# Packed attention and gated MLP on one core: batch 2's attention held behind batch 0's last gate, batch 1's parts laid out again, weights narrowed later

## The chip, the cores and the metric

The kernel runs on one NeuronCore of a Trainium2 chip. Its engines are TensorE (PE, matmuls; "PEld" is its weight load), VectorE (DVE), ScalarE (ACT), GpSimd (POOL) and SyncE (SP, whose queue "SPq" issues all DMAs here). Each engine works through its own queue in order; a waiting instruction holds up all behind it. Time is device microseconds (us) of the whole kernel; the figure compared is the median over runs.

## The reference

Eight batches, eight heads, 576 tokens, head size 64. For each batch and head, 32 packed queries `p` attend to `k` and `v`; then every token's `q` attends to the 32 packed results, which serve as keys and values. The result, turned to tokens x 512, goes through a gated MLP with 2048 inner features.

```python
def sm_attn(qq, kk, vv):
    s = scale * np.matmul(qq, kk.transpose(0, 1, 3, 2))
    s = s - np.max(s, axis=-1, keepdims=True)
    a = np.exp(s)
    a = a / (np.sum(a, axis=-1, keepdims=True) + 1e-09)
    return np.matmul(a, vv)
p_packed = sm_attn(p, k, v)
out = sm_attn(q, p_packed, p_packed)
# x = out as (4608, 512)
h = x @ w_in
g = h * np.clip(h + 3.0, 0.0, 6.0) / 6.0
return g @ w_out
```

The two weight matrices arrive as 64-bit floats, so their words are loaded as pairs of 32-bit integers and turned into 32-bit floats on the chip ("narrowed").

## The kernel before

**Folding.** The second attention's product with the packed values is folded into the MLP: `m = p_packed x w_in` is made per batch (for batch 0 in `u_m0`, 128 inner features at a time; for the others in `u_m`, 512 at a time), and the first product is `m` times the attention weights `a`. Both are split into a high and a low part (`m_hi`, `m_lo`, `a_hi`, `a_lo`), so a first product is three matmuls for each of two head groups. The gate follows: a Relu on ACT (L994 for batch 0), min and multiply on DVE (L995). The second product multiplies the gated tile with w_out.

**Three stages.** `first_attention` (from L499) does batch 0's attention, with an order written out by hand. `first_moe` (from L934) does batch 0's MLP in 16 steps, one for each 128 inner features, and carries three other things between its matmuls: loading the weights, narrowing them, and batch 1's attention. Then a loop over batches 1 to 7 does each batch's MLP with the next batch's attention in between (`moe`, `fill`, `attention`); it uses w_out split into a high and a low part (`split_w_out`, L173 on ACT and L175 on DVE).

**A step f of `first_moe`**, on PE: 12 matmuls of the first product (`gemm1`, L491), 8 of `u_m0(f+1)` (L207), then 8 of the second product of step f-1 (L947). The first product's PSUM tile has one buffer, so step f+1's first product waits for step f's gate on DVE; it also waits for `m_lo(f+1)` (L220, DVE, after `m_hi`, L218, ACT). `u_m0` and all parts of batch 1's attention share two PSUM banks (`att_ps`), and a half of `s1` or `s2` takes both.

**Narrowing** (`narrowed`, L131) of one 128x512 tile is two operations on ACT (L143, L145), two on DVE (L151, L153) and an add on POOL (L157). w_in(f) must be narrowed before `u_m0(f)`, w_out(f) before the second product of f. Raw tiles of w_in have three buffers, those of w_out two; tiles 2 and 3 have places of their own. `w_in_step` and `w_out_step` are generators: `step(x, n)` takes n operations of one, `rest(x)` all that are left.

**Batch 1's attention** is the table that `first_parts` (L452) returns: a row for each step, with three places: before the first product, after the gate, and after the second product. `ld` issues four DMAs (L227) for one pair of heads into one of two `nat` buffers, `tn` turns such a tile on DVE (L406) and so frees the buffer; `load_p` issues four (L247), `load_v` five (L263). `s1` (scores of the packed queries, softmax), `et` (transposes of the weights), `pv` (their product with v), `ppt` (transpose of the result) and `s2` (scores of all queries, softmax, turn, split) are generators of which each `go` takes the next piece.

**What sets the order.** Inside `first_attention` and `first_moe` the order on PE, DVE, ACT and POOL is the program's; in `first_moe` on SP too. What is traced outside (batch 2's attention, the splits of w_out, most of batch 1's MLP) is placed by a planner, which works with estimated times and puts such instructions between the hand-ordered ones where it thinks an engine is free. `tc.issue_after(ins)` keeps every instruction of its block that runs on the engine of `ins` behind `ins` in that engine's queue. `first_moe` returns `gate`, the last step's two gate instructions, and the splits are held behind them.

The three spots around which the prediction turns:

```python
rest(in_(f + 2))                       # L990, ahead of the gate
gate = [nc.scalar.activation(...)]     # L994
gate.append(nc.vector.scalar_tensor_tensor(...))   # L995
if f:
    rest(m_(f + 1))
attend(f, 1)
rest(out_(f + 1), out_(f + 2))
```

## Time and profile before

| what | value |
|---|---|
| time, median of 3 runs (lowest to highest) | 778.28 us (777.43 to 779.56) |
| profiled execution, time of its own | 780.75 us |
| its span, first to last instruction | 778.9 us |
| mean granted clock of PE | 0.987 |
| busy: PE, weight loads, DVE, ACT, POOL | 751.4, 575.6, 359.7, 378.0, 252.9 us |
| DMA: packets, bytes | 191203, 55.95 MB |
| first instruction of batch 1's first product (L864) on PE | 162.79 us |

A timeline row reads: start, length, engine, line, operation, output<-inputs, shapes, count, and in brackets how long the engine had stood idle before it and what released it. A row of groups gives the count, then busy us and mean ns, then the idle time before them. Times inside the span are from its start.

### The profile page before, as it was taken

The page shows a single profiled execution, that of the slowest core. Times are in us where ns is not written, and L with a number is a line of the kernel's source. Part 1 is how long each engine was busy: PE and PEld are TensorE (multiplying, and loading weights), DVE is VectorE, ACT ScalarE, POOL GpSimd, SP SyncE. Part 2 cuts the span into 40 slices and gives each one's busy share as a digit, 9 for nine tenths or more (in the row PEclk, how much of TensorE's full clock was granted, in tenths as well). Part 3 has the DMA queues.
Part 4 walks back from the last instruction along what each step waited for, and adds up shares of the span by engine and source line. Part 5 has one row for each costly group of instructions (what it writes and reads, how often), then busy time and mean ns, then how long its engine had stood idle before and what let it go on. Part 6 is the DMA issues. An engine that isn't in the chain of part 4 may idle for free.

```text
span 778.9 us, 13851 instructions
## 1 busy us (share of the span) xinstructions
PE 751.4 (96%) x5133; PEld 575.6 (74%) x5133; DVE 359.7 (46%) x746; ACT 378.0 (49%) x906; POOL 252.9 (32%) x399
## 2 busy tenths in 40 slices
PE   8899987989999999999999999999999999999998
PEld 6654554457867887778877887778777887788886
DVE  4595758673265337333462337333462337231111
ACT  4365743574445545454354545454354545553343
POOL 0353432222323223433243232433243223443332
PEclk9799998999999999999999999999999999999999
DMA  8739696011440254005230254005230120000010
GB/s 253 216 115 242 162 250 126 1 55 31 96 90 13 50 102 90 2 14 106 50 87 1 51 103 89 1 13 108 51 86 1 46 44 28 1 26 4 1 41 27
DMA packets 191203, 55.95 MB, mean 72 GB/s; under 512 B 173216, under 2 KB 184480, under 8 KB 191136
## 3 DMA queue, kind: packets, MB, share of 16 engines
q1 hardware_dynamic: 191136, 55.08, 30.9%
q8 instruction: 40, 0.66, 0.4%
q14 instruction: 27, 0.22, 0.1%
HBM read 45.61 MB, written 9.44 MB: 71 GB/s over the span
## 4 chain that ended last, share of the span: by engine, by line
PE 81%; DMA 6%; DVE 6%; SPq 3%; issue 2%; ACT 2%; DVEq 0%; ACTq 0%
PE acc L893 44%; PE ps_hh L864 23%; PE ps L277 6%; PE acc L947 3%; DMA nat<-in_k_dram 2%; DMA v_nat<-in_v_dram 2%; PE ps L331 1%; PE ps_h L491 1%; SPq L227 1%; DMA raw_in<-in_moe_w_in_dram 1%; PE ps L315 1%; DVE tr L406 1%; DMA nat<-in_q_dram 1%; PE ps_w L679 1%; DVE t L995 1%
## 5 line engine op out<-in xcount | busy, mean ns | idle before, releaser
L893 PE MATMUL acc<-wo_hi,g 128*128 128x512 f32 x896 | 316.8, 395 | 0.8 <-ACT g L881 0.8
L882 POOL TENSOR_TENSOR g<-t,g 128x256 fp32r<-128x256 f32 x224 | 166.7, 747 | 413.3 <-ACT g L881 391.4
L877 DVE SCALAR_TENSOR_TENSOR t<-t,ps_hh 128x320 f32<-128x320 f32 (+1 forms) x224 | 100.3, 449 | 247.5 <-ACT t L876 247.4
L876 ACT ACTIVATE t<-ps_hh,three 128x320 f32<-128x320 f32 (+1 forms) x224 | 112.6, 503 | 178.9 <-PE ps_hh L864 169.8
L893 PEld LDWEIGHTS acc<-wo_hi,g 128*128 128x128 f32 x896 | 167.7, 188 | 35.4 <-issue 3.5
L893 PE MATMUL acc<-wo_lo,g 128*128 128x512 f32 x448 | 177.7, 397 | 0.0
L864 PE MATMUL ps_hh<-a_hi,m_hi 128*128 128x320 f32 (+1 forms) x448 | 136.9, 306 | 3.2 <-issue 3.2
L881 ACT CAST g<-t 128x256 fp32r<-128x256 f32 x224 | 90.5, 405 | 95.7 <-DVE t L877 94.6
L864 PE MATMUL ps_hh<-a_lo,m_hi 128*128 128x320 f32 (+1 forms) x448 | 133.4, 298 | 0.0
L864 PE MATMUL ps_hh<-a_hi,m_lo 128*128 128x320 f32 (+1 forms) x448 | 133.2, 297 | 0.0
L864 PEld LDWEIGHTS ps_hh<-a_hi,m_hi 128*128 128x128 f32 x448 | 84.9, 190 | 37.4 <-issue 24.2
L893 PEld LDWEIGHTS acc<-wo_lo,g 128*128 128x128 f32 x448 | 84.5, 189 | 13.5 <-issue 3.4
L864 PEld LDWEIGHTS ps_hh<-a_lo,m_hi 128*128 128x128 f32 x448 | 85.0, 190 | 8.6 <-issue 1.4
L864 PEld LDWEIGHTS ps_hh<-a_hi,m_lo 128*128 128x128 f32 x448 | 85.0, 190 | 1.3 <-issue 0.9
L947 PE MATMUL acc<-wo_x,t 128*128 128x512 f32 x128 | 60.4, 615 | 0.0
L406 DVE STREAM_TRANSPOSE tr<-nat 128x576 f32<-128x576 f32 x56 | 41.9, 765 | 29.6 <-PE ps L277 14.3
L399 DVE TENSOR_TENSOR m_lo<-ps,m_hi 128x512 fp32r<-128x512 f32 x56 | 36.1, 684 | 32.0 <-ACT m_hi L398 32.0
L947 PEld LDWEIGHTS acc<-wo_x,t 128*128 128x128 f32 x128 | 23.7, 195 | 27.3 <-issue 27.3
L888 POOL TENSOR_TENSOR bnd_lo<-t,bnd_hi 128x64 fp32r<-128x64 f32 x112 | 39.1, 349 | 0.0
L157 POOL TENSOR_TENSOR w_in_sb<-w_in_sb,raw_in 128x512 int32<-128x512 int32 x14 | 18.1, 1292 | 48.9 <-DVE w_in_sb L153 44.2
L398 ACT CAST m_hi<-ps 128x512 fp32r<-128x512 f32 x56 | 29.9, 589 | 8.1 <-PE ps_hh L864 8.1
L277 PE MATMUL ps<-w_in_sb,pps 64*32 64x512 f32 x448 | 33.4, 601 | 0.0
(166 smaller groups left out, 790.9 us busy)
## 6 DMA issues: line engine op xcount, KB each, us to landing
out_dram<-osb SPq DMA_DIRECT2D x36, 256.0 KB, 2.2
nat<-in_k_dram SPq DMA_DIRECT2D x112, 72.0 KB, 2.5
nat<-in_q_dram SPq DMA_DIRECT2D x112, 72.0 KB, 2.5
raw_in<-in_moe_w_in_dram SPq DMA_DIRECT2D x14, 512.0 KB, 5.1
raw_out<-in_moe_w_out_dram SPq DMA_DIRECT2D x14, 512.0 KB, 5.6
v_nat<-in_v_dram SPq DMA_DIRECT2D x56, 128.0 KB, 2.9
spare<-in_k_dram SPq DMA_DIRECT2D x2, 512.0 KB, 4.8
raw<-in_moe_w_in_dram SPq DMA_DIRECT2D x2, 512.0 KB, 6.2
```

Of the source, the lines that this page charges most:

```text
L277: nc.tensor.matmul(banks[x][NPK * a:NPK * a + NPK, :n], rows[half, a], c, start=True, stop=True)
L398: nc.scalar.copy(out=hi[:, x], in_=ps)
L399: nc.vector.tensor_sub(out=lo[:, x], in0=ps, in1=hi[:, x].bitcast(F32))
L406: nc.vector.transpose(out=t, in_=state.pop(("nat", which, b, a)))
L864: nc.tensor.matmul(h[:, :n], mm[:, g, fs], aa[:, t0:t0 + n], start=(g == 0 and i == 0), stop=(g == NG - 1 and i == 2),)
L876: nc.scalar.activation(out=t[:, :n], in_=h, func=AF.Relu, bias=three)
L877: nc.vector.scalar_tensor_tensor(out=t[:, :n], in0=t[:, :n], scalar=6.0, in1=h, op0=ALU.min, op1=ALU.mult)
L881: nc.scalar.copy(out=gh, in_=tm)
L882: nc.gpsimd.tensor_sub(out=gl, in0=tm, in1=gh.bitcast(F32))
L888: nc.gpsimd.tensor_sub(out=bnd_lo[:, slot:slot + REM], in0=tb, in1=bh.bitcast(F32))
L893: nc.tensor.matmul(acc, gg, ww, start=(f == 0 and i == 0), stop=(f == NF - 1 and i == 2),)
L947: nc.tensor.matmul(accs[i], t[:, i * P:(i + 1) * P], wo_x[f], start=(f == 0), stop=(f == NF - 1),)
```

## The change

1. Batch 2's attention, traced in batch 1's MLP, is held behind `gate`, and `gate` now also holds the last weight load of `first_moe`. So its ACT, DVE and SP instructions come after the last gate's Relu, the last gate's multiplication and the load of w_out(15).
2. The table of batch 1's parts has another layout: at most one group of matmuls a step, placed after the second product; loads and turns of k come one step earlier, the softmax of `s2` later.
3. In a step of `first_moe` the gate and `m_lo(f+1)` come ahead of the narrowing of w_in(f+2) and w_out.
4. `first_attention` no longer narrows w_out(0), w_out(1) and w_in(2). Those of w_out(0) and w_out(1), and w_in(2), move into step 0 after its gate; from there w_out(2) goes to step 1, w_out(3) and w_out(4) to step 2, and w_out(f+2) to the later ones. w_in(1) is narrowed later within `first_attention`, and `u_m0(1)` with its cast comes after the first product of step 0. Two warm-up matmuls of eleven go.

```diff
@@ -26,7 +26,7 @@
 SPLIT_AHEAD = 4
 
 
-WARM = (3, 2, 2, 1, 3)
+WARM = (3, 2, 2, 2)
 
 
 @with_exitstack
@@ -463,19 +463,23 @@
         def go(part):
             return lambda: next(part, None)
 
+        def more(x):
+            return lambda: load_v(b, x)
+
         return [
-            [[], [lambda: load_p(b), ld("k", 0)], [ld("k", 1)]],
-            [[], [], [lambda: transpose_p(b), tn("k", 0), ld("k", 2)]],
-            [[tn("k", 1)], [], [ld("k", 3)]],
-            [[tn("k", 2)], [], [lambda: load_v(b, 0)]],
-            [[tn("k", 3)], [go(s1)], [go(s1), ld("q", 0)]],
-            [[go(s1)], [go(s1)], [go(s1), ld("q", 1)]],
-            [[go(et[0])], [go(et[0])], [go(pv[0]), tn("q", 0), ld("q", 2)]],
-            [[go(pv[0])], [go(et[1])], [go(et[1]), tn("q", 1), lambda: load_v(b, 1), ld("q", 3)]],
+            [[lambda: load_p(b), ld("k", 0), ld("k", 1)], [], [lambda: transpose_p(b), tn("k", 0), ld("k", 2)]],
+            [[], [], [tn("k", 1), ld("k", 3)]],
+            [[], [tn("k", 2)], [more(0)]],
+            [[], [tn("k", 3)], [go(s1), ld("q", 0)]],
+            [[], [], [go(s1), ld("q", 1)]],
+            [[go(s1)], [go(s1)], [go(s1), go(et[0]), go(et[0])]],
+            [[tn("q", 0)], [ld("q", 2)], [go(pv[0]), go(et[1])]],
+            [[go(et[1])], [go(pv[0]), tn("q", 1)], [more(1), ld("q", 3)]],
             [[tn("q", 2)], [], []],
-            [[go(pv[1])], [go(pv[1])], [tn("q", 3)]],
-            [[go(ppt)], [go(ppt)], [go(s2)]],
-            [[go(s2)], [go(s2)], [go(s2)]],
+            [[], [], [go(pv[1])]],
+            [[go(pv[1])], [tn("q", 3)], [go(ppt)]],
+            [[go(ppt)], [], [go(s2)]],
+            [[], [], [go(s2)]],
             [[go(s2)], [go(s2)], [go(s2)]],
             [[go(s2)], [go(s2)], [go(s2)]],
             [[go(s2)], [go(s2)], []],
@@ -788,7 +792,7 @@
         r1 = next(a1)
         step(tq[1])
         qt.append(next(tq[1]))
-        win0, wout0 = w_in_step(0), w_out_step(0)
+        win0 = w_in_step(0)
         pv_ps = wide()
         pack(0, *et0, r0, v0)
         step(win0)
@@ -799,10 +803,9 @@
         qtr = [turned_rest((q0, q1), act)]
         b0, b1 = s2(0), s2(1)
         m0, m1 = u_m0(0, tail), u_m0(1, tail)
-        win1, wout1 = w_in_step(1), w_out_step(1)
+        win1 = w_in_step(1)
         step(b0)
         rest(win0)
-        step(win1, 2)
         step(b0, 3)
         pack(1, *et1, r1, v1)
         step(tq[2])
@@ -810,7 +813,6 @@
         qt.append(next(tq[2]))
         step(tq[3])
         qtr.append(turned_rest((q2, q3), act))
-        rest(win1)
         rest(pt1)
         qt.append(next(tq[3]))
         step(b0, 4)
@@ -820,23 +822,19 @@
         step(b1, 3)
         rest(m0)
         rest(b0)
-        step(m1, 2)
-        rest(wout0)
-        win2 = w_in_step(2)
-        step(win2, 2)
+        step(win1, 2)
         warm(WARM[1])
         h = ps_h0.tile([P, 2, 512], F32, name="ps_h0", tag="w")
         gemm1(h, 0, 0)
         step(b1, 4)
+        rest(win1)
         warm(WARM[2])
         step(b1, 2)
+        rest(b1)
+        gemm1(h, 0, 1)
+        step(m1, 2)
         warm(WARM[3])
-        rest(m1)
-        rest(b1)
-        rest(wout1)
-        gemm1(h, 0, 1)
-        warm(WARM[4])
-        return h, {2: win2}, {1: wout1}
+        return h, {}, {}, m1
 
     HAND = {mybir.EngineType.PE, mybir.EngineType.DVE, mybir.EngineType.Activation, mybir.EngineType.Pool}
     pend = []
@@ -931,10 +929,10 @@
                 pend.append(gemm2)
                 second(2)
 
-    def first_moe(h, w_in, w_out):
+    def first_moe(h, w_in, w_out, m1):
 
         plan = first_parts(1) if B > 1 else []
-        accs, m0 = [], {}
+        accs, m0 = [], {1: m1}
 
         def attend(f, place):
             for part in plan[f][place] if f < len(plan) else ():
@@ -987,16 +985,16 @@
                 for g in range(NG):
                     gemm1(h, f, g)
                 step(m_(f + 1))
-            rest(in_(f + 2))
             hv = h[:, :, :HS]
             t = gp.tile([P, S], F32, name="t")
             tv = t.rearrange("p (a n) -> p a n", a=2)
             gate = [nc.scalar.activation(out=tv, in_=hv, func=AF.Relu, bias=three)]
             gate.append(nc.vector.scalar_tensor_tensor(out=tv, in0=tv, scalar=6.0, in1=hv, op0=ALU.min, op1=ALU.mult))
-            if f:
-                rest(m_(f + 1))
+            rest(m_(f + 1))
             attend(f, 1)
-            rest(out_(f + 1), out_(f + 2))
+            rest(in_(f + 2))
+            for i in (range(2), (2,), (3, 4))[f] if f < 3 else (f + 2,):
+                rest(out_(i))
             slot = slice(bnd_slot(f), bnd_slot(f) + REM)
             nc.scalar.copy(out=bnd_hi[:, slot], in_=t[:, 4 * P:])
             nc.gpsimd.tensor_sub(out=bnd_lo[:, slot], in0=t[:, 4 * P:], in1=bnd_hi[:, slot].bitcast(F32))
@@ -1008,7 +1006,7 @@
             u_m(1, 0)
         gemm2(*last)
         hand.close()
-        return gate
+        return gate + [state["load"]]
 
     stage = ExitStack()
     wp = stage.enter_context(tc.tile_pool(name="wp", bufs=2))
@@ -1044,9 +1042,12 @@
                 u_m(*late.pop(0))
             elif c == 1 and f % FPC == 0 and f >= FPC and soon:
                 u_m(*soon.pop(0))
-            for _ in range(PER_STEP if s < NF + FPC - 1 else 1000):
-                if next(ahead, ahead) is ahead:
-                    break
+            with ExitStack() as behind:
+                for ins in gate if b == 1 else ():
+                    behind.enter_context(tc.issue_after(ins.ins))
+                for _ in range(PER_STEP if s < NF + FPC - 1 else 1000):
+                    if next(ahead, ahead) is ahead:
+                        break
         for c in range(2):
             moe(b, (c,), lambda f, c=c: fill(c, f))
     with tc.manual_schedule(engines={mybir.EngineType.PE}):
```

## The prediction

> **What bounds the kernel now.** I read the page, then the busy time by stretches, then each engine's timeline from 14 to 165 us. The page's first line gives the span; in a row of stretches the columns are start:end, length, busy us of TensorE (PE), weight loads, VectorE (DVE), ScalarE (ACT) and GpSimd (POOL), then the granted clock, the DMA share and GB/s.
>
> ```profile
> span 778.9 us, 13851 instructions
> ```
>
> ```profile
> 50.10:104.20 54.10, 52.20 (x348) 31.00 (x347) 37.66 (x70) 30.14 (x63) 23.91 (x24) 1.00 0.84 201
> 104.20:123.50 19.30, 14.68 (x89) 8.16 (x88) 12.57 (x24) 7.09 (x15) 5.90 (x6) 0.91 1.15 230
> 123.50:148.50 25.00, 19.46 (x85) 11.49 (x84) 19.26 (x32) 11.11 (x24) 7.67 (x7) 0.93 0.23 47
> 148.50:162.80 14.30, 11.15 (x63) 5.09 (x61) 10.29 (x17) 12.04 (x25) 1.25 (x4) 0.98 0.01 2
> 162.80:251.00 88.20, 88.20 (x615) 67.41 (x616) 41.73 (x88) 39.95 (x102) 24.58 (x43) 0.98 0.29 63
> ```
>
> From 162.8 us on PE is busy all the time (88.20 of 88.20 in batch 1's MoE, and the six later ones are like it): 616 us that only fewer matmuls could shorten, and the change has the same ones. What can move lies ahead of 162.8 us: the opening up to batch 0's first gate, its 16 steps, and the hand-over to batch 1. The boundaries above are the starts of the first products of steps 2, 10, 12 and 15 and of batch 1's MoE.
>
> A step without stalls has this length:
>
> ```profile
> 50.15 0.69 PE L491 MATMUL ps_h<-a_hi,m_hi 128*128 128x288 f32 x1
> 55.96 0.69 PE L491 MATMUL ps_h<-a_hi,m_hi 128*128 128x288 f32 x1
> ```
>
> That is 5.81 us from step 2's first product to step 3's, with PE busy throughout. Steps 10 to 12 and 12 to 15 take 19.3 and 25.0 us where 2 and 3 such steps are 11.6 and 17.4.
>
> **A. The opening: narrowing of w_in(1), w_out(0), w_out(1), w_in(2) taken out of it.** The rows of ACT, DVE and PE:
>
> ```profile
> 22.77 0.68 ACT L143 ACTIVATE raw_in<-raw_in 128x512 int32<-128x512 uint32 x1 [4.49 <-DMA raw_in<-in_moe_w_in_dram]
> 23.89 0.61 ACT L707 ACTIVATE z<-z 128x512 f32<-128x512 f32 x1
> 32.91 0.63 ACT L707 ACTIVATE z<-z 128x512 f32<-128x512 f32 x1
> 41.90 0.74 ACT L994 ACTIVATE t<-ps_h,three 128x576 f32<-128x576 f32 x1 [0.47 <-PE ps_h L491]
> ...
> 20.56 0.67 DVE L706 TENSOR_TENSOR z<-ps_w,mx 128x512 f32<-128x512 f32 x1
> 25.09 0.45 DVE L357 COPY pp_bd<-ps_t 64x64 f32<-64x64 f32 x2
> 31.05 0.67 DVE L706 TENSOR_TENSOR z<-ps_w,mx 128x512 f32<-128x512 f32 x1
> 38.10 0.96 DVE L723 TENSOR_TENSOR z<-z,dn 128x256 f32<-128x256 f32 x2
> ...
> 17.06 1.10 PE L679 MATMUL ps_w<-pp_bd,qt 128*128 128x64 f32 x8 [0.25 <-DVE pp_bd L357]
> 23.19 0.45 PE L593 MATMUL ps_t<-ident,spare 64*64 64x64 f32 x8
> 25.68 1.81 PE L679 MATMUL ps_w<-pp_bd,qt 128*128 128x64 f32 x8 [2.04 <-DVE pp_bd L357]
> 46.42 0.66 PE L207 MATMUL ps<-w_in_sb,pp_bd 128*64 128x128 f32 x8
> ```
>
> ACT stands 4.49 us on w_in(1)'s landing, with group 0's exponential and two q copies queued behind it; its input was ready at 21.2 (20.56 + 0.67). DVE's pp_bd copy sits behind that narrowing, and PE waits 2.04 us for it. Without it the scores of group 1 start when L593 ends, at 23.6, and at the full clock's 1.10 for eight rather than 1.81 I put their end at 26.5 instead of 30.2. Group 1's subtraction then goes from 31.05 to 27.4 and its exponential from 32.91 to 28.6. The normalising product comes at about 31.3 instead of 38.10, because w_out(0)'s two DVE operations and the wait for them are gone as well. So far 6.8 us. Then u_m0(1) and its cast now stand between the last first product and the gate (0.66 and an estimated 0.4, as long as m_lo in the fence of D), so the gate's Relu goes from 41.90 to 36.4: 5.5 us.
>
> Part of it is given back in step 0, which now narrows w_in(2), w_out(0) and w_out(1) after its gate. A narrowing is 1.1 us on ACT (22.77 to 23.89), a pair on DVE and an add on POOL:
>
> ```profile
> 42.01 1.36 POOL L157 TENSOR_TENSOR w_in_sb<-w_in_sb,raw 128x512 int32<-128x512 int32 x1 [3.23 <-DVE w_in_sb L153]
> 42.25 1.67 DVE L153 SCALAR_TENSOR_TENSOR wo_x<-raw_out,wo_x 128x512 int32<-128x512 int32 x1
> 43.84 0.74 DVE L995 SCALAR_TENSOR_TENSOR t<-t,ps_h 128x576 f32<-128x576 f32 x1
> ```
>
> Gate out at 37.9 (36.4 + 0.74 + 0.74), m_lo(1) 38.3, first product of step 1 at 38.4. w_in(2) leaves POOL at 40.8 (DVE pair 1.1, add 1.3 after 38.3), so u_m0(2) waits 0.6 us for it. w_out(0) leaves POOL at 42.5; the second product of 3.5 us waits for that, and step 2 begins at 46.0 instead of 50.15. The two warm-up matmuls fewer (9 for 11) stand where PE waits for DVE either way: nothing. **Term A: -4.1 us.** Bounds: -6.2 if the wait for POOL vanishes (6.2 is step 1's 44.6 against 38.4), and -1 if every DVE operation of the three is as slow as the 1.67 row (three more us).
>
> [...]
>
> **B. Steps 2 to 10: one PE part a step, gates ahead of narrowing.** Batch 1's parts in this stretch are two halves of s1, two et and two pv:
>
> ```profile
> 66.49 0.71 PE L277 MATMUL ps<-tr,pps 64*32 64x288 f32 x14 [1.38 <-DVE m_lo L220]
> 84.34 0.90 PE L331 MATMUL ps<-v_nat,et 128*32 128x64 f32 x40 [0.28 <-DVE m_lo L220]
> 87.55 0.66 PE L315 MATMUL ps<-ident,e 128*128 128x128 f32 x4
> 91.48 0.27 PE L319 MATMUL ps<-ident,e 128*64 128x128 f32 x1
> ```
>
> Two of each are 2 x (0.71 + 0.66 + 0.27 + 0.90) = 5.1. Eight steps are 46.5, together 51.6 against 54.1 now. The stalls to go are the 1.38 (s1 wanted the bank whose m_lo stood behind a k turn and w_in's narrowing) and smaller ones. Placed after the second product of 3.5 us, each part has m_lo (0.4 us behind the gate) done long before. **Term B: -2.5.** Bounds: 0 if the DMA decides (rival 2), -2.9 if the parts overlap a little as they do now.
>
> **C. Steps 10 to 12: batch 2's attention held.** The stalls and what caused them:
>
> ```profile
> 116.94 0.31 DVE L254 STREAM_TRANSPOSE pps<-p_nat 128x128 f32<-128x128 f32 x1 [4.83 <-DMA p_nat<-in_p_dram]
> ...
> 118.44 1.12 PE L207 MATMUL ps<-w_in_sb,pp_bd 128*64 128x128 f32 x8 [3.77 <-DVE z L367]
> 134.01 0.37 PE L491 MATMUL ps_h<-a_hi,m_hi 128*128 128x288 f32 x1 [4.09 <-ACT raw_out L145]
> ```
>
> DVE stands 4.83 us in front of batch 2's p, and behind it in DVE's queue are s2's copies out of the PSUM banks, w_in's narrowing and the gate; PE waits 3.77 for a bank. After it PE restarts slowly (L207 1.12 against 0.66). With batch 2's DVE work behind gate 15, two steps cost 11.6, the turn of pp 0.27 and one half of s2 0.71: 12.6 against 19.3. **Term C: -6.7.** Bounds: -7, and -3 if only the waits and not batch 2's four k turns (L406 in the next fence, 3.1 us) mattered.
>
> **D. Steps 12 to 15: s2's softmax.** It is DVE's work, now laid into steps 13 to 15. The groups of DVE from 111.5 to 148.5 us (busy us, mean ns):
>
> ```profile
> L376 DVE TENSOR_TENSOR z<-z,mx 128x576 f32<-128x576 f32 x2 | 2.1, 1050 | 0.1
> L380 DVE TENSOR_REDUCE den<-z 128x18 f32<-128x576 f32 x2 | 1.5, 750 | 0.7 <-ACT z L377 0.7
> L406 DVE STREAM_TRANSPOSE tr<-nat 128x576 f32<-128x576 f32 x4 | 3.1, 770 | 1.4 <-DMA nat<-in_k_dram 1.2
> L220 DVE TENSOR_TENSOR m_lo<-ps,m_hi 128x256 fp32r<-128x256 f32 x4 | 1.7, 417 | 0.0
> L153 DVE SCALAR_TENSOR_TENSOR w_in_sb<-raw_in,w_in_sb 128x512 int32<-128x512 int32 x3 | 2.1, 693 | 0.1
> L151 DVE TENSOR_SCALAR w_in_sb<-raw_in 128x512 int32<-128x512 int32 x3 | 1.2, 411 | 1.8 <-ACT raw_in L145 1.8
> ```
>
> Step 13 gives DVE the subtraction 1.05, two reductions and a product at 0.75 each, a turn of the same shape as L406's 0.77 and an estimated 0.6 of small ones (4.7), the gate and m_lo (0.74 + 0.42) and two narrowings at 1.1: 8.1 us against PE's 5.81. u_m0(15) waits for w_in(15), which is behind the softmax, so 2.2 us of stall stay. Three steps, a half of s2 (0.71) and 2.2 are 20.3 against 25.0. **Term D: -4.7.** Bounds: -6.9 without the stall, 0 if the 4.09 us wait stays.
>
> **E. The hand-over.** After gate 15 the w_out splits and batch 1's first weights queue on ACT and DVE:
>
> ```profile
> 151.43 7.37 ACT L173 CAST wo_hi<-wo_x 128x512 fp32r<-128x512 f32 x14
> 162.79 0.60 PE L864 MATMUL ps_hh<-a_hi,m_hi 128*128 128x320 f32 x1 [3.15 <-issue]
> ```
>
> Fourteen casts go before batch 1's first m_hi, and PE idles 3.15 us. In the change gate 15 comes some 4 us later against PE (the turn and cast of s2's second half are ahead of it), but PE's other work covers most. If the casts stay in front, the stretch is 17.2; if the planner puts m_hi first, 11.1. Nothing in the trace decides, so I keep today's 14.3. **Term E: 0**, bounds -3.2 and +2.9.
>
> **F. Batch 2's attention later.** It meets the splits in batch 1's MoE. DVE has 41.73 of 88.2 us there, so the turns (four at 0.77) fit. I allow +1.5 for one short wait on a transfer, here or in step 0 to 4, where ld k2 now stands ahead of w_in(5) and w_out(4) on SP's queue until k0 is turned. Bounds 0 and +4.8, the wait of row L254.
>
> **Sum.** -4.1 -2.5 -6.7 -4.7 + 0 + 1.5 = -16.5. The profiled execution took 780.75 (span 778.9 and 1.85 around it): 764.3 for it. Runs have a median of 778.28, so the forecast for them is **761.8, say 762**.
>
> **Rivals.**
>
> 1. The stall moves. DVE's order in batch 1's MoE is the planner's; if p and two k turns each stand in front of gates as the 4.83 us row did, MoE 1 loses up to 4.83 + 2 x 2.4, about 9.6 us: 778.3 - 18.0 + 9.6 = 770. For it: that row. Against: PE was never idle in 162.8 to 251, although turns waited for transfers there too. Chance 0.12.
>
> 2. The DMA becomes the bound of steps 2 to 10. Its share is 0.84 of 54.1 us, 45.4 us at 16 engines' worth; w_in(5) and w_out(4), sent earlier today, come in (1 MB at 201/0.84 = 239 GB/s, 4.4 us) and batch 2's first k tile goes (1.2): 48.6 of 51.6 us. If transfers can't be packed closer than today's 0.84, it takes 57.9: +6.3, giving 768. Chance 0.13.
>
> 3. Slower: batch 2 comes too late for its own MoE.
>
> ```profile
> 174.54 0.82 DVE L293 TENSOR_REDUCE mx<-ps 128x1 f32<-128x288 f32 x2 [2.90 <-ACT e L292]
> 237.01 1.43 DVE L391 TENSOR_TENSOR a_lo<-at,a_hi 128x576 fp32r<-128x576 f32 x2
> ```
>
> From s1 to a_lo it takes 63.9 us, and 88.2 are there, so s1 may come 24.3 us into MoE 1 (today 11.7). With the turns behind gate 15 (136) and two rounds of loads I expect it 5 to 10 us in, at 150 to 155. Each us beyond 24.3 is lost, and past 24.3 + 18 = 42 us the kernel is slower than before; at 48 us 784. Against it: batch 1's weights are all in by then, and so the queue is empty. Chance 0.07.
>
> **How the numbers follow.** The forecast's own case has 0.63 and the range 755 to 768; rivals 1, 2 and 3 have 0.12, 0.13, 0.07, and 0.05 is left for a change that ends within 0.3% (2.3 us, about what a measurement of this kernel can tell from no change). The low end is all favourable bounds of A and E and no F: -4.1 - 2.1 - 2.5 - 6.7 - 4.7 - 3.2 = -23.3, 755. The high end takes D at 0 and E at +2.9 with F at 1.5: -8.9, 769.4, and rival 1 reaches 770 to 773. So 754.5 to 773. Faster 0.88, same 0.05, slower 0.07.
>
> **What would show it.** A: no 4.49 us wait of ACT in front of L143, first Relu of a gate near 36.4, step 2 near 46. B: no wait of L277 for m_lo. C: no L254 or batch 2 turn on DVE before gate 15, step 12 near 110. D: u_m0(15) waiting some 2 us, step 15 near 130.5. E: batch 1's first product near 145 to 148. F: PE fully busy after it. The forecast is wrong if batch 1's first product comes after 156, or if PE idles more than 5 us in batch 1's MoE.

## The result: 0.6% faster, under a third of what was forecast

| | before | changed kernel |
|---|---|---|
| median of 9 runs each | 779.2 us (777.43 to 782.07) | 774.49 us (771.84 to 777.46) |
| ratio, 95% interval | | 0.994 (0.9921 to 0.996) |
| profiled execution, span | 780.75 us, 778.9 us | 774.74 us, 773.0 us |

The forecast was 762.0 us (754.5 to 773); the gain is 4.7 us where 16.5 were forecast. Batch 1's first product, which was expected near 145 to 148 us, came at 156.97; after 156 was one of the prediction's own signs of being wrong. The first line of the profile after, and its busy time by the stretches that the prediction used, cut at the same instructions (first products of steps 2, 10, 12, 15 and of batch 1's MoE); the columns are those of before:

```profile
span 773.0 us, 13846 instructions
```

```profile
49.31:104.91 55.60, 52.09 (x348) 30.96 (x346) 42.34 (x70) 32.66 (x68) 25.25 (x26) 1.00 0.85 219
104.91:117.47 12.56, 12.56 (x80) 7.27 (x73) 9.36 (x16) 6.80 (x14) 5.71 (x7) 1.00 0.58 167
117.47:137.95 20.48, 18.05 (x108) 10.73 (x101) 16.54 (x27) 8.92 (x18) 7.71 (x9) 1.00 0.41 87
137.95:156.97 19.02, 11.34 (x62) 4.92 (x61) 15.15 (x26) 13.49 (x27) 1.03 (x2) 0.91 0.36 58
156.97:245.00 88.03, 86.93 (x613) 66.74 (x614) 45.65 (x92) 40.12 (x100) 27.07 (x43) 0.98 0.30 64
```

Steps 10 to 12 are full now (12.56 of 12.56 us busy, 19.30 long before), and steps 12 to 15 went from 25.00 to 20.48. But step 2 begins at 49.31, only 0.84 earlier than before; steps 2 to 10 grew from 54.10 to 55.60, and the hand-over from 14.30 to 19.02. What follows batch 1's first product takes 616.0 us, as before. What TensorE (PE) waited for between 30 and 160 us, as total, times and longest ("issue" means nothing that the profile shows):

```profile
PE ps_hh L862 <- issue: 6.9, 1, 6.9
PE ps L207 <- POOL w_in_sb L157: 4.3, 3, 2.4
PE ps_h L495 <- ACT m_hi L218: 2.8, 1, 2.8
PE ps L207 <- DVE mx L293: 1.5, 1, 1.5
```

Two of these waits stand where the prediction expected none or a short one: 2.8 us at step 1 and 6.9 us in front of batch 1's first product. Step 1 first, in the timeline after:

```profile
35.27 0.74 ACT L991 ACTIVATE t<-ps_h,three 128x576 f32<-128x576 f32 x1 [1.72 <-PE ps_h L495]
35.91 0.67 ACT L143 ACTIVATE raw<-raw 128x512 int32<-128x512 uint32 x1
...
38.63 0.64 ACT L145 ACTIVATE raw_out<-raw_out 128x512 f32<-128x512 f32 x1
39.17 0.36 ACT L218 CAST m_hi<-ps_t 128x256 fp32r<-128x256 f32 x1
...
39.58 0.40 PE L495 MATMUL ps_h<-a_hi,m_hi 128*128 128x288 f32 x1 [2.76 <-ACT m_hi L218]
44.62 5.26 PE L945 MATMUL acc<-wo_x,t 128*128 128x512 f32 x8 [0.91 <-POOL wo_x L157]
```

The gate's Relu came at 35.27, 1.1 us earlier than the forecast 36.4. But ScalarE then ran all six narrowing instructions of w_in(2), w_out(0) and w_out(1), and only after them, at 39.17, the cast m_hi(1) for which step 1 waits. The cast is issued at the end of the opening, the narrowing at the start of batch 0's MoE. The MoE's instructions are held only behind the last load, the last a_hi and the last a_lo of the opening, so nothing keeps them behind m_hi(1). The hand-over:

```profile
143.15 0.67 ACT L389 CAST a_hi<-at 128x576 fp32r<-128x576 f32 x1 [2.81 <-DVE at L386]
143.73 0.73 ACT L991 ACTIVATE t<-ps_h,three 128x576 f32<-128x576 f32 x1
144.37 7.36 ACT L173 CAST wo_hi<-wo_x 128x512 fp32r<-128x512 f32 x14
...
151.78 1.14 ACT L173 CAST wo_hi<-wo_x 128x512 fp32r<-128x512 f32 x2
152.82 2.02 ACT L398 CAST m_hi<-ps 128x512 fp32r<-128x512 f32 x4
...
146.07 1.39 DVE L406 STREAM_TRANSPOSE tr<-nat 128x576 f32<-128x576 f32 x2
...
151.13 0.78 DVE L406 STREAM_TRANSPOSE tr<-nat 128x576 f32<-128x576 f32 x1 [0.70 <-DMA nat<-in_k_dram]
...
156.19 1.88 DVE L399 TENSOR_TENSOR m_lo<-ps,m_hi 128x512 fp32r<-128x512 f32 x3
...
156.97 0.61 PE L862 MATMUL ps_hh<-a_hi,m_hi 128*128 128x320 f32 x1 [6.94 <-issue]
```

Gate 15's Relu runs 5.8 us after step 15 began (2.3 before), because the cast of s2's second half stands in front of it. Then 16 split casts, not the 14 that the prediction counted, go ahead of batch 1's m_hi, and on VectorE (DVE) batch 2's k turns, two of them waiting for transfers, go between the splits and m_lo. The same casts stood there before:

```profile
150.79 0.74 ACT L994 ACTIVATE t<-ps_h,three 128x576 f32<-128x576 f32 x1 [2.26 <-PE ps_h L491]
...
159.88 2.02 ACT L398 CAST m_hi<-ps 128x512 fp32r<-128x512 f32 x4
```

From gate 15's Relu to m_hi it takes 9.1 us in both kernels. So of the 4.7 us that the hand-over grew by, 3.5 are the later gate, and the other 1.2 come between m_hi and the first product (4.15 us, 2.91 before), where DVE now has batch 2's turns among the splits.

### The profile page after: what moved, and what is told of

Read it like the earlier page. It is cut to its first block, busy times and chain, and to the rows that moved or that the text cites. A ratio compares the mean times of both kernels' runs of the same rounds, so it can differ in the third digit from the quotient of the medians.

```text
span 773.0 us, 13846 instructions
## 1 busy us (share of the span) xinstructions
PE 745.1 (96%) x5129; PEld 571.1 (74%) x5129; DVE 367.2 (48%) x746; ACT 377.9 (49%) x906; POOL 254.5 (33%) x399
## 4 chain that ended last, share of the span: by engine, by line
PE 80%; DVE 6%; ACT 3%; issue 2%; DMA 1%; SPq 1%; DVEq 0%; ACTq 0%
PE acc L891 44%; PE ps_hh L862 23%; PE ps L277 6%; PE acc L945 3%; PE ps L331 2%; PE ps_h L495 1%; DVE wo_x L153 1%; PE ps L315 1%; DVE tr L406 1%; DMA nat<-in_k_dram 1%; DMA raw_out<-in_moe_w_out_dram 1%; PE ps L207 1%; SPq L227 1%; DVE z L376 1%; ACT t L991 0%
## 5 line engine op out<-in xcount | busy, mean ns | idle before, releaser
L399 DVE TENSOR_TENSOR m_lo<-ps,m_hi 128x512 fp32r<-128x512 f32 x56 | 36.1, 684 | 31.7 <-ACT m_hi L398 31.7
L157 POOL TENSOR_TENSOR w_in_sb<-w_in_sb,raw_in 128x512 int32<-128x512 int32 x14 | 19.3, 1378 | 57.3 <-DVE w_in_sb L153 34.3
```

The costliest lines, as they stand in the source:

```text
L399: nc.vector.tensor_sub(out=lo[:, x], in0=ps, in1=hi[:, x].bitcast(F32))
```

## The experiments

Each kernel was timed beside the kernel before on the same chip. Before's own median was 776.9 to 779.2 from one group of runs to the next, so the ratios are what is compared; 0.001 is 0.78 us. The changed kernel was timed in the first group only. In the table "opening" is the start of step 2, the next three are the prediction's stretches, "after" is the time from batch 1's first product to the end of the span, and these five come from one profile each. The profiled execution is the fastest of the kernel's runs in some (e1, e7, e12, e13) and the slowest in others (e6, e8, e11, e14, e15), so small differences between rows of stretches mean little.

| kernel | us | ratio (95%) | opening | 2-10 | 10-15 | hand-over | after |
|---|---|---|---|---|---|---|---|
| before | 779.2 | 1 | 50.15 | 54.1 | 44.3 | 14.3 | 616.1 |
| changed | 774.49 | 0.994 (0.9921-0.996) | 49.31 | 55.6 | 33.0 | 19.0 | 616.0 |
| e4 hold alone | 772.86 | 0.9935 (0.9913-0.9957) | 45.95 | 53.8 | 39.7 | 15.1 | 615.8 |
| e13 hold and table | 768.62 | 0.9893 (0.9875-0.991) | 45.91 | 54.9 | 31.9 | 17.8 | 615.3 |
| e6 table undone | 783.84 | 1.008 (1.0062-1.0097) | 50.40 | 55.4 | 46.3 | 15.1 | 615.7 |
| e10 gates undone | 767.96 | 0.9868 (0.9851-0.9884) | 45.45 | 54.2 | 31.9 | 17.8 | 616.3 |
| e5 opening undone | 769.88 | 0.9911 (0.9892-0.9931) | 49.04 | 54.4 | 33.0 | 18.4 | 614.9 |
| e1 m_hi(1) first | 771.25 | 0.9921 (0.9894-0.9949) | 44.86 | 55.6 | 33.0 | 18.3 | 616.0 |
| e2 splits behind m_lo | 771.84 | 0.9933 (0.9912-0.9954) | 47.51 | 54.8 | 36.1 | 10.5 | 621.8 |
| e3 both | 769.58 | 0.9898 (0.9864-0.9932) | 45.38 | 55.3 | 36.1 | 10.5 | 622.3 |
| e7 splits held step by step | 763.11 | 0.9821 (0.9799-0.9842) | 44.60 | 55.6 | 33.0 | 11.5 | 615.0 |
| e8 gate 15 first | 771.28 | 0.9922 (0.9902-0.9942) | 49.66 | 55.0 | 34.7 | 15.6 | 616.6 |
| e9 k2 later | 772.95 | 0.9927 (0.9911-0.9943) | 48.62 | 54.8 | 36.1 | 15.2 | 616.1 |
| e11 = e7 with gate 15 first | 762.29 | 0.9796 (0.9779-0.9812) | 44.83 | 56.2 | 33.0 | 10.5 | 616.4 |
| e12 = e7, opening undone | 764.11 | 0.9827 (0.9808-0.9846) | 46.27 | 54.5 | 33.0 | 11.5 | 615.6 |
| e14 = e7, gates undone | 762.24 | 0.9798 (0.9775-0.9821) | 44.10 | 54.5 | 31.9 | 11.6 | 619.3 |
| e15 = e13, splits step by step | 763.11 | 0.9826 (0.9803-0.9849) | 49.48 | 55.6 | 31.8 | 11.6 | 615.9 |

**First group: the two new waits, and the hold by itself.** In e1 only the matmuls of u_m0(1) stay in the opening; its cast is issued by batch 0's first step, behind the Relu:

```diff
-        step(m1, 2)
+        step(m1, 1)
         warm(WARM[3])
```

> The changed kernel with the cast m_hi(1) put behind the first gate's Relu on ScalarE, ahead of the narrowing of w_in(2), w_out(0) and w_out(1). Theory (the 2.76 us wait of step 1 and what follows from it is the missing part of term A): m_hi(1) ends near 36.4 us, step 1 starts at 37.2 instead of 39.58, step 2 at 46.9 instead of 49.31, and the kernel takes 772.3 us instead of 774.5 (2.2 less). Rival 1 (the transfers set steps 2 to 6): step 2 starts earlier, but step 5 stays at 70.5 and step 10 at 104.9, because ScalarE waits that much longer for w_in(5) and w_out(4), and the time stays 774.5. Rival 2 (the narrowings get in each other's way in step 0, whenever it starts): step 1 at 37.2, step 2 still after 48.5, time 774.

Steps 1 and 2 start at 36.42 and 44.86, and the time is 771.25 us. In the profile the rivals fall: step 10 comes at 100.42 instead of 104.91, so nothing takes the gain back on the way. In the times the gain is smaller: 1.5 us by ratios against the changed kernel, and 2.7 for the same edit between e2 and e3, both with intervals that overlap. In the profile step 2 gains 4.5 us, of which 0.5 is an opening that already ran ahead by that much; more than the 2.4 expected, because in this execution one wait brought a second loss with it:

```profile
35.39 0.36 ACT L218 CAST m_hi<-ps_t 128x256 fp32r<-128x256 f32 x1
36.42 0.37 PE L495 MATMUL ps_h<-a_hi,m_hi 128*128 128x288 f32 x1
41.72 3.70 PE L945 MATMUL acc<-wo_x,t 128*128 128x512 f32 x8 [1.38 <-POOL wo_x L157]
```

The eight second products take 3.70 us; in the changed kernel, after PE's 2.76 us wait, 5.26, at a granted clock of 0.50 to 0.55 up to 48 us.

In e2 and e3 the w_out splits and batch 2's attention wait for u_m(1, 0)'s last m_hi and m_lo, which u_m now returns, and not for gate 15:

```diff
-            u_m(1, 0)
+            gate = u_m(1, 0)
```

> The changed kernel with the w_out splits and batch 2's attention held behind the last cast and subtraction of batch 1's first weights (m_hi, m_lo) instead of behind gate 15. Theory (at the hand-over the 14 split casts and batch 2's turns stand in front of m_hi and m_lo): the wait of 6.94 us in front of batch 1's first product falls to 1 or less, that product starts at 150.5 to 151.5 us instead of 156.97, and the kernel takes 768.5 us (6 less). Rival 1 (gate 15, late by 3.5 us behind the second half of s2, sets the hand-over): the first product starts at 154 or later and the time is 772 or more. Rival 2 (the work held back is missed in batch 1's MoE): the first product comes near 151, but what follows takes 618 to 622 us instead of 616.0.

> Both edits together. If the two losses are separate, their gains add up: 774.5 - 2.2 - 6.0 = 766.3 us, first product of batch 1 near 148.7. If the transfers set steps 2 to 6, the opening's gain is lost on the way and it takes what the second edit alone takes, near 768.5.

The wait in front of batch 1's first product is gone (hand-over 10.5 us), and the times still fell only by less than 1 us and by 3 us against the changed kernel, going by ratios, whose intervals overlap with its own. Rival 2 of e2 is right: what follows takes 621.8 and 622.3 us. In e3 the loss stands 7 us later:

```profile
150.30 0.78 DVE L406 STREAM_TRANSPOSE tr<-nat 128x576 f32<-128x576 f32 x1 [0.43 <-DMA nat<-in_k_dram]
152.60 0.78 DVE L406 STREAM_TRANSPOSE tr<-nat 128x576 f32<-128x576 f32 x1
153.87 1.28 DVE L399 TENSOR_TENSOR m_lo<-ps,m_hi 128x512 fp32r<-128x512 f32 x2
154.61 2.55 PE L277 MATMUL ps<-w_in_sb,pps 64*32 64x512 f32 x16 [5.01 <-DVE m_lo L399]
```

The products of the next part of batch 1's weights want a PSUM bank whose m_lo stands behind the same splits and turns. The stall moved; nothing had been taken out of its way.

e4 is before with the hold alone:

```diff
-        return gate
+        return gate + [state["load"]]
...
+            with ExitStack() as behind:
+                for ins in gate if b == 1 else ():
+                    behind.enter_context(tc.issue_after(ins.ins))
```

> The kernel before with batch 2's attention held behind gate 15 and the last weight load, and nothing else of the change. Theory (term C is the hold's alone): no VectorE wait in front of the turn of p, steps 10 to 12 take 12.7 to 14 us instead of 19.3, and steps 12 to 15 stay near 25 since s2's softmax remains where it was; the hand-over stays at 14.3; the time is 771.5 to 773 us. Rival (the hold costs at the hand-over what it saves, batch 2's turns standing there beside the splits): steps 10 to 12 shorter by 5 to 7, the hand-over longer by 3 to 5, time 776 to 778.

772.86 us: the hold by itself is worth as much as the whole change. Steps 10 to 12 take 14.0 us, steps 12 to 15 25.7 and the hand-over 15.1, close to the theory. But its opening, in code that is the same as before's, was 4.2 us shorter. Of before and of e4:

```profile
22.00:30.00 8.00, 5.96 (x45) 5.20 (x45) 2.80 (x8) 3.04 (x7) 2.86 (x5) 0.74 0.98 325
30.00:36.00 6.00, 5.92 (x30) 4.60 (x30) 3.64 (x9) 4.15 (x10) 0.00 (x0) 0.50 0.50 83
```

```profile
22.00:30.00 8.00, 7.29 (x75) 5.68 (x72) 5.63 (x16) 4.72 (x13) 2.86 (x5) 1.00 0.95 322
30.00:36.00 6.00, 3.52 (x20) 2.47 (x18) 4.56 (x11) 2.79 (x6) 1.82 (x2) 1.00 0.73 119
...
21.20 0.70 ACT L143 ACTIVATE raw_in<-raw_in 128x512 int32<-128x512 uint32 x1 [3.18 <-DMA raw_in<-in_moe_w_in_dram]
24.15 1.08 PE L679 MATMUL ps_w<-pp_bd,qt 128*128 128x64 f32 x8 [0.17 <-DVE pp_bd L357]
```

In before's profile ScalarE could begin on w_in(1) at 22.77, PE waited 2.04 us for pp_bd, and its granted clock was 0.74 and then 0.50. In e4's it began at 21.20, PE waited 0.17 us, and the clock stayed at 1.00. The opening of before was profiled six times in all: w_in(1) in use by 21.3 us and step 2 near 46 (e4, e12, e13), or at 21.8 to 22.8 and step 2 at 49.0 to 50.2 (before, e5, e15, where the clock fell to 0.77 or less). The prediction had read one of the late ones.

**Second group: the other parts undone one at a time, and two repairs.**

e5, the changed kernel with before's opening (its narrowings and its 11 warm-up products; what is finished or begun is handed to batch 0's steps):

```diff
-        win1 = w_in_step(1)
+        win1, wout1 = w_in_step(1), w_out_step(1)
         step(b0)
         rest(win0)
+        step(win1, 2)
...
-        return h, {}, {}, m1
+        return h, {2: win2}, {0: wout0, 1: wout1}, m1
```

> The changed kernel with the opening of before (w_in(1), w_out(0), w_out(1) and half of w_in(2) narrowed ahead of the first gate, 11 warm-up products). Theory (the opening of before was only as long as 50.15 us in the profile because w_in(1) landed late and TensorE's granted clock fell to 0.5; with the same code it took 45.95 in the run with the hold alone, so the changed opening with its 49.31 is the longer one): step 2 begins near 46 us, and the kernel takes 771 to 772.5 us instead of 774.5. Rival (term A of the prediction, the changed opening saves 1 to 4 us): with the old one back the time is 775.5 to 778.5.

769.88 us, 4.6 less than the changed kernel and 2.3 less by ratios, whose intervals overlap a little. Its profile shows the late case of the opening (49.04), so it can't show a gain. The times exclude the 1 to 4 us that the rival gave the changed opening: as written, putting the narrowing off did not pay. That it cost something is likely, but not clear of noise.

e6, before's table in place of the new one:

```diff
-            [[lambda: load_p(b), ld("k", 0), ld("k", 1)], [], [lambda: transpose_p(b), tn("k", 0), ld("k", 2)]],
-            [[], [], [tn("k", 1), ld("k", 3)]],
+            [[], [lambda: load_p(b), ld("k", 0)], [ld("k", 1)]],
+            [[], [], [lambda: transpose_p(b), tn("k", 0), ld("k", 2)]],
...
```

> The changed kernel with the table of before, in which batch 1's attention is laid into batch 0's 16 steps. Theory (the new table's gain in steps 12 to 15, 4.6 us, is lost again at the hand-over and in steps 2 to 10): steps 12 to 15 take 25 us again instead of 20.4, the hand-over 14.5 to 15.5 instead of 19.0, steps 2 to 10 54 instead of 55.6, and the time is 773 to 775.5 us. Rival (the new table carries its own gain): the time goes up by 3 to 5, to 777.5 to 779.5.

783.84 us, slower than before and far beyond both expectations. Its waits of PE from 30 to 170 us begin with this line, against 4.3 us in the changed kernel:

```profile
PE ps L207 <- POOL w_in_sb L157: 9.1, 5, 3.0
```

So gates ahead of narrowing, put on the old table, make u_m0 wait for w_in five times; the new table leaves three such waits, 4.3 us. This led to e10 below.

e8, the second half of s2's turn and cast behind gate 15:

```diff
-            [[go(s2)], [go(s2)], []],
+            [[], [go(s2), go(s2)], []],
```

> The changed kernel with the second half of s2's turn and cast put behind gate 15 instead of ahead of it. Theory (the 14 casts start with gate 15 and m_hi comes 8.4 us after they begin, so an earlier gate brings everything forward by as much): gate 15's Relu goes from 143.73 to about 141 us, batch 1's first product from 156.97 to 154, and the time from 774.5 to 771.5. Rival (a_hi and a_lo of the second half, now behind the gate, become late behind the casts): the first product stays at 156.5 or later, time 774.5 or more.

Gate 15's Relu came 2.3 us after step 15's start (5.8 in the changed kernel) and the hand-over took 15.6 us instead of 19.0. Not all of that is the edit's: in this profile step 15 began late, after slow products (see the last section), and e9, without this edit, has a hand-over of 15.2 in the same way. From step 10 to batch 1's first product it is 50.26 us here, 51.35 in e9 and 52.06 in the changed kernel. The 771.28 us fit the theory; by ratios they are 1.4 us below the changed kernel, with intervals that overlap.

e7 has the edits of e1 and e2 and, besides, issues each step's u_m ahead of its splits, and holds the splits and batch 2's attention behind that u_m:

```diff
             s = c * NF + f
+            if late:
+                gate[:] = u_m(*late.pop(0)) + gate[-1:]
             if b == 1 and c == 0:
...
                         split_w_out(i)
-            if late:
-                u_m(*late.pop(0))
```

> The kernel of both edits, in which each step's w_out splits and batch 2's attention are held behind the m_hi and m_lo made in that same step of batch 1's MoE (its first three steps make the second to fourth part of batch 1's weights), so that no split stands ahead of them. Theory (the 5.01 us wait in front of the third part's product was the hand-over's loss moved by 8 us: a PSUM bank whose m_lo stood behind splits and turns on VectorE): no wait over 1.5 us between 145 and 165 us, what follows batch 1's first product takes 616 to 617 us, and the kernel 764 to 766 us. Rival (14 splits and 4 turns must be done somewhere before the second products can go, whatever the order): the wait turns up in front of the first second products, as a wait for wo_hi or wo_lo, and the time stays at 768 to 770.

763.11 us, ratio 0.9821, a little better than the theory and 6.0 us below e3 by ratios, with intervals that don't touch; the rest takes 615.0 us. The same place in its timeline:

```profile
140.65 2.18 ACT L398 CAST m_hi<-ps 128x512 fp32r<-128x512 f32 x4
142.72 2.71 ACT L173 CAST wo_hi<-wo_x 128x512 fp32r<-128x512 f32 x5
144.68 0.71 PE L862 MATMUL ps_hh<-a_hi,m_hi 128*128 128x320 f32 x1
```

Four m_hi casts first, five splits (those of the first five steps) after them, and no wait in front of the first product. The splits needed no earlier place: the second products never waited for them.

**Third group.** e9 sends batch 1's third k tile one step later:

```diff
-            [[lambda: load_p(b), ld("k", 0), ld("k", 1)], [], [lambda: transpose_p(b), tn("k", 0), ld("k", 2)]],
-            [[], [], [tn("k", 1), ld("k", 3)]],
+            [[lambda: load_p(b), ld("k", 0), ld("k", 1)], [], [lambda: transpose_p(b), tn("k", 0)]],
+            [[ld("k", 2)], [], [tn("k", 1), ld("k", 3)]],
```

> The changed kernel with the load of batch 1's third k tile sent one step later, so that on SyncE's queue w_in(5) and w_out(4) go ahead of it. Theory (ScalarE's waits of 1.75 and 1.48 us for raw_out, and behind them u_m0(5)'s 1.50 us for mx, come from weights that stood behind this load for 11 us): these waits are gone, steps 2 to 10 take about 54 us instead of 55.6, and the kernel 773 us (1.5 less). Rival 1 (these steps wait for VectorE and POOL in any order): the 1.50 is replaced by another wait of that size and the time stays at 774.5. Rival 2: the turn of the third k tile becomes late for s1, and the time is over 775.

On SyncE's queue in the changed kernel, and in ScalarE's timeline:

```profile
28.57 19.39 SPq L227 DMA_DIRECT2D nat<-in_k_dram  x12
48.07 0.43 SPq L128 DMA_DIRECT2D raw_in<-in_moe_w_in_dram  x1
...
56.87 0.69 ACT L143 ACTIVATE raw_out<-raw_out 128x512 int32<-128x512 uint32 x1 [1.75 <-DMA raw_out<-in_moe_w_out_dram]
61.78 0.69 ACT L143 ACTIVATE raw_out<-raw_out 128x512 int32<-128x512 uint32 x1 [1.48 <-DMA raw_out<-in_moe_w_out_dram]
```

w_in(5) waits at 48.07 behind a k load that waits for a buffer. In e9 both waits of ScalarE are gone, but u_m0(5) still waits 0.95 us for mx (1.50), and steps 2 to 10 take 54.8 us. So the lateness of these weights is real. It is worth 0.8 us in that stretch and 1.0 by ratios, where 772.95 us can't be told from the changed kernel.

e10 puts each narrowing of w_in back in front of its gate:

```diff
+            rest(in_(f + 2))
             hv = h[:, :, :HS]
...
             attend(f, 1)
-            rest(in_(f + 2))
```

> The changed kernel with each step's narrowing of w_in ahead of its gate again, as before. Theory (with the gate ahead, w_in's narrowing ends later, which is what u_m0 waits for: 1.33 us before step 8's and 2.43 us before step 15's in the changed kernel): these two waits are gone or under 0.5, waits of 1 to 1.5 us for a gate (DVE t) appear in their place in the steps in which VectorE has most to do, and the time is 773 to 775. Rival (term B as predicted, the gate ahead is worth its stalls): second products wait for gates in most steps, and the time is 777 or more.

767.96 us, 5.6 less than the changed kernel by ratios, and the intervals don't touch: both expectations were too high, and the theory's waits for gates in exchange did not come (0.5 us in two waits). The groups of DVE from 30 to 150 us, of before, of the changed kernel and of e10:

```profile
L995 DVE SCALAR_TENSOR_TENSOR t<-t,ps_h 128x576 f32<-128x576 f32 x15 | 11.2, 744 | 1.5 <-ACT t L994 1.5
L153 DVE SCALAR_TENSOR_TENSOR wo_x<-raw_out,wo_x 128x512 int32<-128x512 int32 x14 | 10.7, 763 | 0.5
```

```profile
L992 DVE SCALAR_TENSOR_TENSOR t<-t,ps_h 128x576 f32<-128x576 f32 x16 | 11.9, 746 | 15.4 <-ACT t L991 15.4
L153 DVE SCALAR_TENSOR_TENSOR wo_x<-raw_out,wo_x 128x512 int32<-128x512 int32 x14 | 21.5, 1534 | 0.5
```

```profile
L993 DVE SCALAR_TENSOR_TENSOR t<-t,ps_h 128x576 f32<-128x576 f32 x16 | 12.0, 749 | 5.5 <-ACT t L992 5.4
L153 DVE SCALAR_TENSOR_TENSOR wo_x<-raw_out,wo_x 128x512 int32<-128x512 int32 x14 | 10.7, 762 | 0.5
```

With the gate ahead, DVE stands idle for the Relu in nearly every step (15.4 us in all, 1.5 before); the narrowing of w_in used to fill that time. Then w_in's and w_out's narrowing follow each other on DVE, and w_out's second operation falls on POOL's add for w_in. The means in the rows mix two kinds: the operation takes 0.69 us by itself, and 1.65 to 1.74 us where it starts while POOL's add is running. That is so for 14 of its 16 executions in the changed kernel, and for one each before and in e10. By the rows above, the idle time and the slow operations come to 13.9 + 10.8 us of DVE. What slows the operation during the add is not shown. The prediction had the 1.67 us row of before and allowed for more of them in the opening only, in term A's bound of -1.

Less of this reaches PE. In e10's profile 3.9 us of the gain stand in the opening, where step 1's wait is 1.72 us instead of 2.76 and the clock stays at 1.00 behind it, 1.4 in steps 2 to 10, 1.2 in steps 10 to 15 and 1.2 at the hand-over.

Three more kernels join edits. e11 is e7 with e8's row, e12 is e7 with e5's opening:

> The kernel with the splits held step by step, and the second half of s2's turn and cast behind gate 15. Theory (at the hand-over nothing waits for gate 15 any more but u_m(1,0), by 0.75 us): the time is 762 to 763.1 us, against 763.1 without this edit. Rival (the gate is still ahead of everything there): as in the changed kernel, some 3 us less, 760.

> The kernel with the splits held step by step, and the opening of before in place of the new one with m_hi(1) first. Theory (the old opening is as good as the mended new one except where w_in(1) lands late): the time is 761.5 to 763.5 us in the median, with a wider spread of runs than 763.1 (761.5 to 765.9). Rival (the opening as the change means it does save what it should once m_hi(1) is in its place): 765 us or more.

762.29 us: the time is the theory's, that gate 15 no longer sets the hand-over, and the hand-over is 1.0 us shorter. By ratios e11 is 1.9 us below e7, between theory and rival, and the intervals overlap. 764.11 us: a little above its range, and not told from e7's 763.11 by ratios (0.9827, 0.9821). So the old opening and the mended new one can't be told apart in time: putting the narrowing off gained nothing that this pair can see.

**Last group: are the losses one or several?** e13 is before with the hold and the new table, e14 is e7 with e10's order, e15 is e13 with e7's order of splits; their edits are those shown.

> The kernel before with the hold and the new table alone: the opening and the order of gate and narrowing stay as before. With one of the two undone in the changed kernel it takes 769.9 (opening) and 768.0 us (gates). Theory (both cost the same microseconds, those of steps 0 and 1, where the narrowing of w_in(2), w_out(0) and w_out(1) stands behind a gate and a late m_hi(1)): 767 to 769 us. Rival (two separate losses that add up): 774.5 - 4.6 - 6.5 = 763.4 us.

> The kernel with the splits held step by step and m_hi(1) first, with each step's narrowing of w_in ahead of its gate. Theory (what the gate ahead costs outside the opening and the hand-over, both mended here, is 1.4 us in steps 2 to 10 and 1.1 us in steps 12 to 15): 760 to 761 us, step 2 near 44.5, steps 12 to 15 19.3. Rival (all of the 6.5 us come back here too): 756.5 to 758.

> The kernel before with the hold, the new table and the splits held step by step. Theory (the same hand-over gain as in the changed kernel, where it took 6 to 7 us off): 760 to 762 us, no wait in front of batch 1's first product. Rival (gate 15 comes later here, behind the narrowing, and takes the hand-over's gain): 764 us or more.

e13 takes 768.62 us, as the theory of one shared loss has it, and not 763.4: what opening and gates cost is largely the same time. Against the changed kernel that is 3.7 us less by ratios, with intervals that don't touch; 2.3 (e5) and 5.6 (e10) would add up to 7.9. So two of the change's four parts cost together as much as the new table had brought (3.3 us, e4 against e13).

e14 takes 762.24 us, 1.2 to 2.2 more than expected. Its batch 1 begins at 142.09, the earliest of all, but PE then waits 2.66 us for a gate's DVE half at 148.09, and the rest takes 619.3 us: what was won ahead is in part lost in the first steps of batch 1's MoE. This profile is the slowest of its five runs. e15 takes 763.11 us, 5.2 less than e13 by ratios. The hand-over's loss is there without the other two, and the same edit mends it. Whether e8's row helps e14 was not run, nor was the table without the hold.

Two pairs qualify what e5 and e12 say of the opening. With the gates behind the narrowing the new opening is the shorter one by ratios: 2.0 us (e10 against e13) and 2.2 us (e14 against e15), each with intervals that overlap. So a small gain from putting the narrowing off may be there once the gates stay where they were; these runs don't settle it.

e11 and e14, at 762.3 and 762.2 us, are the best of these kernels: 2.0% below before and 1.4% below the changed kernel. Their intervals overlap with e7's.

## Why the prediction was wrong

**The sum.** Against the profiled spans the terms measured -0.8 (A), +1.5 (B), -6.7 (C), -4.5 (D), +4.7 (E) and -0.1 (F), together -5.9 us, where -4.1, -2.5, -6.7, -4.7, 0 and +1.5 were forecast. C and D were right; A, B and E missed by 3.3, 4.0 and 4.7, F by 1.6 the other way.

**A, the opening: wrong in two steps.** "u_m0(1) and its cast now stand between the last first product and the gate": the cast m_hi(1) did not come where the code puts it, but behind six narrowing instructions, since the planner was free to order two blocks that nothing ties (e1). The Relu came 1.1 us earlier than forecast (the working's own terms give 5.7 us, not 5.5), but step 1 began at 39.58 instead of 38.4, and it lasted 9.7 us instead of 7.6, in part at a granted clock of 0.50 to 0.55. The size was wrong too: the 50.15 us came from an execution in which w_in(1) landed late and PE ran at 0.50 to 0.74 of its clock. The prediction read the 1.81 us row as a slowness that the change would cure, but without the change half the profiles don't have it. Against the undisturbed opening of 46 us the changed one is 3.3 us longer, and the mended one (44.1 to 45.4) 0.6 to 1.9 us shorter, which e12's time does not confirm and e14 against e15 leaves open.

**B, steps 2 to 10: wrong in sign.** The stalls named there went, and others took their place: 1.50 us for mx, 1.33 us for w_in, 0.68 us in step 7. With PE's 52.09 us busy, these 3.5 us make up the 55.60; the forecast's 51.6 had room for none. The gate ahead of the narrowing was costed at nothing ("done long before", it says of m_lo); it leaves DVE idle for the Relu and puts two narrowings on top of each other, and in e10 the first two waits are gone and the stretch takes 54.2. The third stays there, and 0.81 us in front of u_m0(7) come, both for ScalarE's copy L316. The likely cause is that the table does not keep to one part a step: steps 5 and 6 have two parts after the second product, and step 7 has one ahead of its first product (L319). The bound of 0 on this term excluded a loss without a reason. Rival 2, the DMA, came nearest in size (57.9 for the stretch) but had another cause: e9 finds about 1 us there.

**C, the hold: right.** No turn of batch 2 is on DVE before gate 15, and e4 shows the hold alone: 0.9935, with steps 10 to 12 at 14.0 us.

**D, s2's softmax: right in size**, with the stall that it forecast: 2.2 us, measured 2.43 on w_in(15). e10 shows that the stall was not the softmax alone but the gate's place: there the three steps take 19.3 us.

**E, the hand-over: the doubt was named and decided wrongly.** "If the casts stay in front, the stretch is 17.2; if the planner puts m_hi first, 11.1. Nothing in the trace decides, so I keep today's 14.3." The casts stayed in front, as they were before, and it took 19.0, over the bound by 1.8; e7's 11.5 is the other end. "PE's other work covers most" of the late gate was wrong: the gate came 3.5 us later against PE, and all of it is in the hand-over. Batch 2's turns, which this term left out, stand in the other 1.2. How much an earlier gate alone wins back is less sure: e8 is 1.8 us shorter from step 10 on and 1.4 by ratios. A value between two ends with a mechanism each is a value that no mechanism gives.

**F and the other rivals.** Batch 2's later start cost nothing after the first product (616.0 against 616.1 us), so rivals 1 and 3 did not come.

## What to carry to other kernels

A hold costs nothing to test alone: here one part of four carried the gain, and two gave the third's away. Before an instruction is moved ahead of another, look at what filled the time in which its engine waited for its input, and at which pair of operations becomes neighbours behind it. And where two blocks of a fixed order meet, tie the instruction that the next product waits for, not only the last of each kind; else a planner puts cheap bulk work in front of it.

## What the runs showed of the hardware that was not expected

A short wait of PE cost twice in some profiles. All ten profiles of the new table with the gates ahead of the narrowing have the same wait of about 2.4 us at u_m0(15) (2.43 in the changed kernel, 2.42 in e8). In six of them the products after it ran at the usual speed (eight of 128x512 in 3.70 us); in four (e2, e3, e8, e9) they took 5.03 to 6.34 us. In the changed kernel after that wait, and in e3 (the granted clock is the third figure from the end):

```profile
134.00:138.00 4.00, 3.77 (x17) 1.93 (x17) 3.26 (x6) 1.57 (x3) 1.75 (x3) 1.00 0.00 0
```

```profile
129.90:136.80 6.90, 6.87 (x17) 3.20 (x17) 5.34 (x9) 2.39 (x5) 1.89 (x3) 0.53 0.01 2
```

The same 17 instructions take 6.9 us at a granted clock of 0.53, 3.1 us more than at 1.00 and on top of the wait itself. Not all of that reaches the total: in e9 the hand-over behind it is shorter by more, since batch 1's first product waits for what follows gate 15 and not for PE. A reduced clock followed the gap of 2.04 us in before's opening (0.50 from 26 to 36 us), four of the ten gaps of 2.4 us at u_m0(15) (0.53 in e3), and all five gaps of 2.8 us at step 1 (the changed kernel, where it was 0.50 to 0.55 from 44 to 48 us, e2, e6, e8, e9). So the length of the gap alone did not decide it at u_m0(15), and what did is not shown.

A load that landed 0.5 to 2 us later moved the opening by 3 to 4 us by this path: w_in(1) late, DVE's pp_bd behind its narrowing, PE idle over 1 us (2.04 in before, 1.19 in e5), clock down (from 22 to 30 us 0.74 and 0.70, against 1.00 in e4, e12 and e13).
